# B step of a two-layer-type kernel: where the V-tail matmuls stand, which engine makes Pm, and what the last steps issue

## The chip, the cores and the metric

The kernel runs on one core of a Trainium2 chip. A core has TensorE (PE; its weight loads, PEld, are listed apart since they overlap the matmuls), VectorE (DVE), ScalarE (ACT), GpSimd (POOL) and SyncE (SP), which here only issues DMAs. The metric is device time in microseconds (us) for one execution of the whole program. Engines run their own instruction streams in order and meet through semaphores.

## The reference

The program applies four layers to x of 2048 tokens by 640: A, B, A, B, each as x + layer(layernorm(x)). Layer A is a linear-memory attention in 4 segments of 512 tokens and 32 heads of 20. Layer B, which the change touches, is a transformer with a recurrent memory: 64 segments of 32 tokens, and 8 memory rows that go from segment to segment.

```python
for s in range(n_seg):                       # 64
    xs = x[:, s * 32:(s + 1) * 32, :]
    h = jnp.concatenate([mem, xs], axis=1)   # 8 + 32 rows
    q, k, v = h @ Wq, h @ Wk, h @ Wv         # 32 heads of 128
    scores = where(mask, q @ k.T * scale, -1e9)
    o = (softmax(scores) @ v) @ Wo
    mem = o[:, :8, :]
    outs.append(o[:, 8:, :])
```

So a segment's rows can be projected ahead of time, but its 8 memory rows are known only when the segment before is through all of attention and the output projection. That recurrence sets the order of everything in B.

## The kernel before, in words

Layer B is one Python loop over 64 steps (`for s in range(nsteps)` in `layer_B`), unrolled. In every B layer the order of TensorE, ScalarE, VectorE and GpSimd is the order in which the code issues the instructions: a wrapper (`_OrdNC`) chains each engine's instructions, which is also why all of them carry line 105 in the profile. The DMA issues on SP are placed by the framework's scheduler. An engine may run ahead of the others into a later step as far as its inputs are there.

The columns of step s. A "thin" operand of 32 columns holds the 8 memory rows that enter segment s and the first 24 tokens of segment s + 1. Its projections Ka, Qa, Kb, Qb and Va, Vb (`thin_mm`: 20 matmuls each, four side by side in column groups of 32, five chunks of 128 of the 640 inputs) give the memory rows' K, Q, V for this step and the 24 tokens' K, Q, V for the next.

The tails. The last 8 tokens of each segment are projected apart, for 8 segments (one group T) at a time, as 64 columns. Eight units per group, one per step, make Q and K for 8 heads each (`tail_unit`: 40 matmuls; `tail_evac` stores to DRAM as QKd), and eight V-tail units make V (`vtail_unit`: five chunks of 4 matmuls of 256 columns, side by side; `vtail_evac` stores to VTd). A step reads back its own part: `tails_load` brings Q and K of the tails into the tile tl (one buffer), GpSimd copies them to QZ and KT (`tails_copy`), and `vtails_in` loads V. In a step s the unit is that of group (s + 1) // 8 + 1; from step 55 on there is no further group, so steps 55 to 63 of each B layer have no unit.

One step, in order of issue on TensorE: Ka, Qa, Kb, Qb; transposes TPak, TPaq, TPbk, TPbq of their copies; the scores (tiles SP, in two groups a and b, preceded by a matmul that adds the mask); Va, Vb; the first 6 of the 8 tail heads; the transposes of the probabilities (PTP, by matmul with an identity, from two tiles: Px for the 32 token columns, Pm for the 8 memory columns); the last 2 tail heads; P times V (OTP); half a chunk of the deferred output projection (OPSd); the output projection OPS (64 matmuls); the other half of OPSd; and the turn.

The softmax runs beside Va, Vb and the tails: VectorE takes the maxima and subtracts them, ScalarE makes the exponentials E, VectorE sums them, takes the reciprocals rs and multiplies: first Pm (12 groups of 8), then Px (groups 0 to 7, then 8 to 11). PTPa needs groups 0 to 7, PTPb groups 0 to 3 and 8 to 11. ScalarE copies PTPa to PTa, VectorE PTPb to PTb.

The turn puts the new memory rows into the next thin operand: ScalarE copies OPS to msb in three parts, TensorE sums and transposes each by tiny matmuls (MT), VectorE copies each MT into the first 8 columns of HX, and the next Ka can begin with chunk 0 as soon as the first copy is there. Between the three MT groups the code issues the five chunks of the V-tail unit as 2, 1 and 2 (`vtail_some`).

PSUM: five buffers (`b_ps`) go round for all tiles named here except TPbq and the tail unit (which share one), OPS and OPSd.

GpSimd has little in a step: the copies QZ (two) and KT of `tails_copy`, the copy OTdef of the attention output for the deferred projection, and now and then a tiny power for the layer norm.

Of the kernel before, what the change touches and what calls it, by code (L numbers as in the profile page):

```python
# [29 lines left out]
NCH = 5  # L30
# [512 lines left out]
def layer_B(nc, tc, C, W, x_src, xb_src, x_dst, mem0, B_Wv, B_Wo, nsteps=64, out_bf16=False, tag=""):  # L543
    SCB = 1.0 / math.sqrt(128.0)
    nc_raw = nc
    nc = _OrdNC(tc, nc_raw, engines=ORDER_ENGINES)
    NG = nsteps // 4
    NT = nsteps // 8
    QKd = tc.dram_tile([nsteps, 128, 512], BF16, name=f"b_QKd{tag}")
    VTd = tc.dram_tile([nsteps, 8, 4096], BF16, name=f"b_VTd{tag}")  # L550
    with ExitStack() as ctx:
# [21 lines left out]
        def ps_tile(shape, dtype, name):  # L573
            return pp.tile(shape, dtype, name=name, tag="ps")


        Px = st.tile([128, 12, 32], BF16, name="b_Px")
        Pm = st.tile([128, 12, 32], BF16, name="b_Pm")
# [39 lines left out]
        def evac(eng, dst, src, scale=None):  # L618
            if eng == "act":
                if scale is None:  # L620
                    nc.scalar.copy(dst, src)
                else:
                    nc.scalar.activation(out=dst, in_=src, func=ACT.Copy, scale=scale)
            else:
                if scale is None:
                    nc.vector.tensor_copy(dst, src)
                else:
                    nc.vector.tensor_scalar(out=dst, in0=src, scalar1=scale, scalar2=None, op0=ALU.mult)
# [12 lines left out]
        def ln_spread(g):  # L641
            xt = ln_xt.pop(g)
            tps = ps_tile([128, NCH, 4, 32], BF16, "b_lntps")
            for c in range(NCH):
                nc.tensor.transpose(tps[:, c, :, :].rearrange("p i t -> p (i t)"), xt[:, 128 * c:128 * c + 128], C.identb[:])
            HX[g] = hp.tile([128, NCH, 4, 32], BF16, name="b_HX", tag="HX")
            T, half = divmod(g, 2)
            if half == 0:
                TX[T] = tx.tile([128, NCH, 8, 8], BF16, name="b_TX", tag="TX")
            nc.scalar.copy(HX[g][:, :, :, 8:32], tps[:, :, :, 0:24])  # L650
            nc.scalar.copy(TX[T][:, :, 4 * half:4 * half + 4, :], tps[:, :, :, 24:32])
# [27 lines left out]
        def alloc_seg(s):  # L679
            QT[s] = w2.tile([128, 32, 32], BF16, name="b_QT", tag="QT")  # L680
            KT[s] = w2.tile([128, 32, 40], BF16, name="b_KT", tag="KT")

        def tails_load(s):
            tl = bx.tile([128, 2, 32, 8], BF16, name="b_tl", tag="tl")
            nc.sync.dma_start(tl[:].rearrange("p a h t -> p (a h t)"), QKd[s])
            return tl
# [14 lines left out]
        def tail_unit(T, k, i0, i1, shared=False):  # L701
            proj, hg = divmod(k, 4)
            Wt = W.wk if proj else W.wq
            if i0 == 0:
                if shared:
                    tail_ps[0] = ps_tile([128, 8, 64], F32, "b_tail")
                else:
                    tail_ps[0] = po.tile([128, 8, 64], F32, name="b_tail", tag="tail")
            ps = tail_ps[0]
            for i in range(i0, i1):  # L710
                h = 8 * hg + i
                for c in range(NCH):
                    nc.tensor.matmul(ps[:, i, :], lhsT=Wt[:, c, 128 * h:128 * h + 128], rhs=TX[T][:, c, :, :].rearrange("p s t -> p (s t)"),
                                     start=(c == 0), stop=(c == NCH - 1))

        def tail_evac(T, k, eng, home=None):
            proj, hg = divmod(k, 4)
            pool_, tg = home or (wk, "tu")
            tu = pool_.tile([128, 8, 8, 8], BF16, name="b_tu", tag=tg)
            evac(eng, tu[:].rearrange("p s h t -> p h s t"), tail_ps[0][:].rearrange("p h (s t) -> p h s t", t=8),  # L720
                 None if proj else SCB)
            o = 256 * proj + 64 * hg
            nc.sync.dma_start(QKd[8 * T:8 * T + 8, :, o:o + 64].rearrange("s p f -> p s f"), tu[:].rearrange("p s h t -> p s (h t)"))

        def vtail_unit(T, k, c0=0, c1=NCH, ps=None):
            b4, ch = divmod(k, 2)
            if ps is None:
                ps = ps_tile([128, 256], F32, "b_vtail")
            for c in range(c0, c1):
                for q in range(4):  # L730
                    n = 2 * b4 + q // 2
                    nc.tensor.matmul(ps[32 * q:32 * q + 32, :], lhsT=TX[T][:, c, 4 * (q % 2):4 * (q % 2) + 4, :].rearrange("p s t -> p (s t)"),
                                     rhs=W.wv[:, c, 512 * n + 256 * ch:512 * n + 256 * ch + 256],
                                     start=(c == 0), stop=(c == NCH - 1), tile_position=(0, 32 * q), skip_group_check=True)
            return ps
# [122 lines left out]
        for s in range(nsteps):  # L858
            last = (s == nsteps - 1)
            u = s + 1  # L860
            cols = cols_of(u)
            unit = None
            if (s + 1) // 8 + 1 < NT:
                unit = ((s + 1) // 8 + 1, (s + 1) % 8)
            if not last:
                alloc_seg(s + 1)
                tl = tails_load(s + 1)
# [41 lines left out]
            E_ = wk.tile([128, 12, 40], BF16, name="b_E", tag="E0")  # L909
# [11 lines left out]
            def soft_sum(a):  # L921
                nc.vector.tensor_reduce(out=ssum[:, slice(*GR[a])], in_=E_[:, slice(*GR[a]), :], axis=AX.X, op=ALU.add)

            def soft_p(P_, k0, k1, g0, g1):
                nc.vector.tensor_tensor(out=P_[:, g0:g1, 0:k1 - k0], in0=E_[:, g0:g1, k0:k1],
                                        in1=rs[:, g0:g1].unsqueeze(2).to_broadcast([128, g1 - g0, k1 - k0]), op=ALU.mult)

            def p_transp(b):
                ptp = ps_tile([128, 2, 4, 40], F32, "b_PTP")
                sel = C.identb[:, 64 * b:64 * b + 64].rearrange("p (i c) -> p i c", c=32)[:, :, 0:16]  # L930
                for part, P_ in ((1, Pm), (0, Px)):
                    nc.tensor.matmul(ptp[:, part, :, 8:40], lhsT=P_[:, 4 + 4 * b:8 + 4 * b, :].rearrange("p g k -> p (g k)"), rhs=C.identb[:],
                                     start=True, stop=True, skip_group_check=True)
                    nc.tensor.matmul(ptp[:, part, :, 0:8], lhsT=P_[:, 0:4, :].rearrange("p g k -> p (g k)"), rhs=sel,
                                     start=True, stop=True, skip_group_check=True)
                return ptp
# [41 lines left out]
            soft_sum(0)  # L978
            soft_sum(1)
            nc.vector.reciprocal(out=rs[:], in_=ssum[:])  # L980
            soft_p(Pm, 32, 40, 0, 12)
            soft_p(Px, 0, 32, 0, 8)
            soft_p(Px, 0, 32, 8, 12)
            if not last:
                tails_copy(s + 1, tl)
            VH[s] = w2.tile([128, 2, 512], BF16, name="b_Vth", tag="Vth")
# [4 lines left out]

            if ln_ready:
                ln_spread(ln_ready.pop(0))
            if unit:
                tail_unit(unit[0], unit[1], 0, 6)
            ptpa = p_transp(0)
            PTa = wk.tile([128, 2, 4, 40], BF16, name="b_PTa", tag="PTa")
            ptpb = p_transp(1)
# [1 line left out]
            for hf in range(2):  # L1000
                for pt, ptp, eng in ((PTa, ptpa, "act"), (PTb, ptpb, "dve")):
                    evac(eng, pt[:, :, 2 * hf:2 * hf + 2, :], ptp[:, :, 2 * hf:2 * hf + 2, :])
            if unit:
                tail_unit(unit[0], unit[1], 6, 8)
                tail_evac(unit[0], unit[1], "act")
            otf = [ps_tile([128, 2, 4, 40] if j else [128, 4, 40], F32, "b_OTP") for j in range(4)]
            ots = {j: (otf[j][:, 0, :, :], otf[j][:, 1, :, :]) for j in (1, 2, 3)}
# [23 lines left out]
            vps, vc = None, 0  # L1031

            def vtail_some(n_):
                nonlocal vps, vc
                if unit and vc < NCH:
                    vps = vtail_unit(unit[0], unit[1], vc, min(NCH, vc + n_), vps)
                    vc = min(NCH, vc + n_)

            if not last:
                dst = cols_of(u + 1)  # L1040
                msb = wk.tile([128, 320], BF16, name="b_msb", tag="msb")
                parts = ((0, 1), (1, 3), (3, NCH))
                for ca, cb in parts:
                    nc.scalar.copy(msb[:, 64 * ca:64 * cb], ops[:, 64 * ca:64 * cb])
                for pi, (ca, cb) in enumerate(parts):
                    mt = ps_tile([128, cb - ca, 8], F32, f"b_MT{pi}")
                    for c in range(ca, cb):
                        for q in range(4):
                            o = 64 * c + 32 * (q % 2)
                            nc.tensor.matmul(mt[32 * q:32 * q + 32, c - ca, :], lhsT=msb[:, o:o + 32], rhs=selm[:, q // 2, :],  # L1050
                                             start=True, stop=True, tile_position=(0, 32 * q), skip_group_check=True)
                    nc.vector.tensor_copy(dst[:, ca:cb, 0:8], mt[:])
                    vtail_some((2, 1, NCH)[pi])
            vtail_some(NCH)
            if unit:
                vtail_evac(unit[0], unit[1], vps, "act")
# [107 lines left out]
```

## Time and profile before

| | us |
|---|---|
| time before, median of 3 runs | 2844.14 (2843.91 to 2844.21) |
| profiled execution, its own time | 2838.53 |
| its span, first to last instruction | 2836.8 |
| first B layer, first Ka to step 63 | 461.2 to 1411.3 |
| second B layer, first Ka to step 63 | 1861.3 to 2811.7 |
| PE busy | 2647.7 (93%) |
| PEld busy | 1679.9 (59%) |
| DVE busy | 1676.7 (59%) |
| ACT busy | 1566.2 (55%) |
| POOL busy | 633.4 (22%) |
| TensorE clock granted, mean | 0.974 |

The profile is of one execution. Starts and durations are in us from the first instruction; an instruction's row names its output and inputs by the program's tiles (`b_` for layer B, `a_` for layer A). In the chain of waits each piece is the work that the end of the run waited for, followed back from the last instruction. In the timeline, the bracket at the end of a row is the engine's idle time ahead of it and who ended that. The granted clock is the share of its full speed that TensorE was allowed. Matmuls are pipelined: a matmul's row covers its passage through the array, and the next can start before it ends, so starts, not ends, give the pace.

### The profile page before, as it was taken

To read this page: it belongs to the slowest core of one execution; us is meant where nothing else is said; L and a number is where in the kernel's file an instruction comes from. 1 tells how busy PE (TensorE), PEld (TensorE's weight loads), DVE (VectorE), ACT (ScalarE), POOL (GpSimd) and SP (SyncE) were. 2 spreads that over 40 slices of the span, in tenths; PEclk is the share of its full clock that TensorE was granted. 3 is DMA by queue.
4 is the path that set the end of the run, shared out by engine and by line. 5 is a ranking of instruction groups with operands and counts; after the bars stand their busy time and mean duration, and the time that the engine had idled before them with its cause. 6 is when DMAs were issued, how large, how long until landed. Compare 5 with 4: busy or idle time off the path is not lost.

```text
span 2836.8 us, 145610 instructions
## 1 busy us (share of the span) xinstructions
PE 2647.7 (93%) x64776; PEld 1679.9 (59%) x64776; DVE 1676.7 (59%) x4682; ACT 1566.2 (55%) x3516; POOL 633.4 (22%) x1506
## 2 busy tenths in 40 slices
PE   5899998999999999999979999889999999999998
PEld 2455555666666666665535555556666666666654
DVE  5778864555555555555468878545555555555554
ACT  3777773555555455544438778545555555555543
POOL 3456651000000000000025665410001000000000
PEclk8999999999999999999979999899999999999999
DMA  5110135122211222111130111531111112111110
GB/s 208 60 44 23 36 127 138 42 44 45 45 42 43 44 45 43 43 39 31 24 121 20 57 44 38 181 88 42 41 41 40 41 42 43 42 39 38 38 26 17
DMA packets 322950, 156.42 MB, mean 55 GB/s; under 512 B 245776, under 2 KB 311056, under 8 KB 319248
## 3 DMA queue, kind: packets, MB, share of 16 engines
q1 hardware_dynamic: 320880, 136.63, 18.9%
q8 instruction: 506, 8.29, 1.3%
q10 hardware_dynamic: 1440, 10.49, 1.0%
q14 instruction: 124, 1.02, 0.1%
HBM read 95.65 MB, written 51.38 MB: 52 GB/s over the span
## 4 chain that ended last, share of the span: by engine, by line
PE 61%; DVE 13%; ACT 5%; issue 3%; DMA 2%; POOL 1%; SPq 0%; ACTq 0%; DVEq 0%; POOLq 0%
PE b_OPS L105 11%; PE b_Ka L105 5%; PE b_Kb L105 5%; PE b_Qb L105 5%; PE b_Qa L105 5%; PE b_SP L105 4%; PE b_OTP L105 4%; DVE b_ssum L105 3%; PE b_vtail L105 2%; PE b_tail L105 2%; DVE b_negmax L105 2%; PE b_PTP L105 2%; PE b_OPSd L105 2%; DVE b_SP L105 2%; ACT b_E L105 2%
## 5 line engine op out<-in xcount | busy, mean ns | idle before, releaser
L105 PEld LDWEIGHTS <-b_HX 128*32 128x32 bf16 x15360 | 441.2, 97 | 339.3 <-issue 17.9
L375 DVE TENSOR_REDUCE a_nm<-a_S 128x2 f32<-128x1024 f32 (+3 forms) x512 | 404.1, 812 | 91.8 <-PE a_T L407 69.7
L410 ACT ACTIVATE a_PT<-a_T 128x1024 bf16<-128x1024 f32 (+1 forms) x384 | 340.9, 891 | 51.0 <-PE a_T L407 45.1
L105 POOL COPY b_OTdef<-b_OTsb 128x256 bf16<-128x256 bf16 x128 | 51.2, 400 | 1330.9 <-ACT b_OTsb L105 1315.0
L105 PE MATMUL b_OPS<-b_wo,b_OTsb 128*32 128x320 bf16 x8192 | 318.4, 307 | 8.3 <-issue 5.8
L105 PEld LDWEIGHTS <-b_OTsb 128*32 128x32 bf16 x8192 | 205.7, 98 | 99.2 <-DVE b_OTsb L105 24.4
L412 POOL TENSOR_SCALAR_AFFINE_SELECT a_PT<-a_PT 128x256 bf16<-128x256 bf16 (+1 forms) x384 | 197.6, 517 | 236.6 <-ACT a_PT L410 235.5
L105 DVE CAST b_HX<-b_MT 128x8 bf16<-128x8 f32 x372 | 62.5, 172 | 279.8 <-PE b_MT L105 264.6
L105 ACT CAST b_msb<-b_OPS 128x64 bf16<-128x64 f32 x378 | 69.3, 256 | 245.8 <-PE b_OPS L105 245.8
L105 ACT CAST b_kq<-b_Kb 128x512 bf16<-128x512 f32 x128 | 74.9, 585 | 202.5 <-PE b_Kb L105 202.5
L105 DVE TENSOR_SCALAR b_kq<-b_Qa 128x512 bf16<-128x512 f32 x128 | 88.6, 692 | 126.0 <-PE b_Qa L105 125.5
L105 DVE COPY b_KT<-b_TPak 128x128 bf16<-128x128 bf16 x128 | 28.8, 225 | 225.6 <-PE b_TPak L105 225.6
L105 PE MATMUL b_Va<-b_wv,b_HX 128*32 128x512 bf16 x2520 | 160.7, 380 | 0.0
L105 PE MATMUL b_Vb<-b_wv,b_HX 128*32 128x512 bf16 x2520 | 160.0, 379 | 0.0
L105 PE MATMUL b_Qb<-b_wq,b_HX 128*32 128x512 bf16 x2520 | 159.0, 379 | 0.0
L105 PE MATMUL b_Kb<-b_wk,b_HX 128*32 128x512 bf16 x2520 | 159.0, 379 | 0.0
L105 PE MATMUL b_Ka<-b_wk,b_HX 128*32 128x512 bf16 x2520 | 159.0, 379 | 0.0
L105 PE MATMUL b_Qa<-b_wq,b_HX 128*32 128x512 bf16 x2520 | 159.0, 379 | 0.0
L407 PE MATMUL a_T<-a_q,a_kT 32*128 32x512 bf16 (+3 forms) x1024 | 139.4, 306 | 20.4 <-DVE a_nm L375 14.7
L105 PEld LDWEIGHTS <-b_kq 128*128 128x128 bf16 x2080 | 116.8, 98 | 69.7 <-ACT b_kq L105 55.2
L366 PE MATMUL a_S<-c_negu,c_identb 128*128 128x128 bf16 (+1 forms) x768 | 124.4, 241 | 25.9 <-DVE a_nm L375 15.4
L105 DVE CAST b_OTsb<-b_OTP 128x160 bf16<-128x160 f32 (+1 forms) x384 | 122.4, 374 | 43.0 <-PE b_OTP L105 42.9
(196 smaller groups left out, 5614.8 us busy)
## 6 DMA issues: line engine op xcount, KB each, us to landing
b_QKd<-b_tu SPq DMA_DIRECT2D x128, 128.0 KB
b_tl<-b_QKd SPq DMA_DIRECT2D x128, 128.0 KB
b_wv<-in_B_Wv_dram SPq DMA_DIRECT2D x10, 1024.0 KB
b_wo<-in_B_Wo_dram SPq DMA_DIRECT2D x16, 640.0 KB
b_VTd<-b_vt SPq DMA_DIRECT2D x256, 32.0 KB
b_Vth<-b_VTd SPq DMA_DIRECT2D x512, 16.0 KB
b_XO<-xres SPq DMA_DIRECT2D x256, 30.0 KB
b_wk<-in_B_Wk_dram ACTq DMA_DIRECT2D x5, 1024.0 KB
```

The lines of the kernel that those rows point to most:

```text
L105: r = f(*a, **k)
L366: nc.tensor.matmul(X[:, e, m0:m1], lhsT=C.identb[:], rhs=C.negu[:, 0:(m1 - m0) // 128, :].rearrange("p a k -> p (a k)"), start=True, stop= ...
L375: nc.vector.tensor_reduce(out=nm[:, qc, 2 * pr:2 * pr + 2], in_=X[:, :, o:o + w_], axis=AX.X, op=ALU.max, negate=True)
L407: nc.tensor.matmul(Y[:, e, o:o + w_], lhsT=kT[rows, 128 * kc:128 * kc + 128], rhs=q2[rows, 128 * kc:512], start=True, stop=True, tile_posi ...
L410: nc.scalar.activation(out=PT[:, :, b:b + width], in_=Y[:, :, 0:width], func=ACT.Exp, scale=SC)
L412: nc.gpsimd.affine_select(out=dv, in_=dv, pattern=[[0, 2], [0, diag], [1, 128]], compare_op=ALU.is_ge, fill=0.0, base=0, channel_multiplie ...
```

## The change

Three things change in a step. First, the V-tail unit's chunks are issued as 2 ahead of the turn, then 1, 1 and the rest (one) behind the three MT groups, where before they were 2, 1 and 2 behind them. Second, Pm is made by GpSimd instead of VectorE, issued between the two Px instructions of VectorE, and the transposes take Px before Pm. On GpSimd's queue Pm stands ahead of the step's `tails_copy`. Third, steps 55 to 62 of each B layer, which have no unit, issue the matmuls of one all the same (the tail heads and the V-tail chunks of unit 0 of the last group); nothing copies or reads what they write.

```diff
             unit = None
             if (s + 1) // 8 + 1 < NT:
                 unit = ((s + 1) // 8 + 1, (s + 1) % 8)
+            work = unit or (None if last else (NT - 1, 0))
...
-            def soft_p(P_, k0, k1, g0, g1):
-                nc.vector.tensor_tensor(out=P_[:, g0:g1, 0:k1 - k0], in0=E_[:, g0:g1, k0:k1],
+            def soft_p(eng, P_, k0, k1, g0, g1):
+                eng.tensor_tensor(out=P_[:, g0:g1, 0:k1 - k0], in0=E_[:, g0:g1, k0:k1],
                                         in1=rs[:, g0:g1].unsqueeze(2).to_broadcast([128, g1 - g0, k1 - k0]), op=ALU.mult)
...
-                for part, P_ in ((1, Pm), (0, Px)):
+                for part, P_ in ((0, Px), (1, Pm)):
...
             nc.vector.reciprocal(out=rs[:], in_=ssum[:])
-            soft_p(Pm, 32, 40, 0, 12)
-            soft_p(Px, 0, 32, 0, 8)
-            soft_p(Px, 0, 32, 8, 12)
+            soft_p(nc.vector, Px, 0, 32, 0, 8)
+            soft_p(nc.gpsimd, Pm, 32, 40, 0, 12)
+            soft_p(nc.vector, Px, 0, 32, 8, 12)
...
-            if unit:
-                tail_unit(unit[0], unit[1], 0, 6)
+            if work:
+                tail_unit(work[0], work[1], 0, 6)
...
+            if work:
+                tail_unit(work[0], work[1], 6, 8)
             if unit:
-                tail_unit(unit[0], unit[1], 6, 8)
                 tail_evac(unit[0], unit[1], "act")
...
-                if unit and vc < NCH:
-                    vps = vtail_unit(unit[0], unit[1], vc, min(NCH, vc + n_), vps)
+                if work and vc < NCH:
+                    vps = vtail_unit(work[0], work[1], vc, min(NCH, vc + n_), vps)
                     vc = min(NCH, vc + n_)
 
+            vtail_some(2)
             if not last:
                 dst = cols_of(u + 1)
...
                     nc.vector.tensor_copy(dst[:, ca:cb, 0:8], mt[:])
-                    vtail_some((2, 1, NCH)[pi])
+                    vtail_some((1, 1, NCH)[pi])
             vtail_some(NCH)
```

## The prediction

> **What bounds the kernel now.** I read the page's slices first: TensorE is 93% busy, and nearly all of the span is the two B layers, 64 steps each. I then took their lengths from the busy time of each engine in stretches cut at the first Ka matmul of a step: steps 0 to 54 of each B layer (they have a tail unit), then steps 55 to 62 (they have none).
>
> ```profile
> 461.20:1288.10 826.90, 810.86 (x23874) 540.77 (x23870) 449.08 (x1457) 429.60 (x1124) 73.72 (x229) 1.00 0.20 43
> 1288.10:1411.30 123.20, 112.39 (x3000) 67.92 (x2992) 62.74 (x205) 54.10 (x145) 9.78 (x32) 0.96 0.12 28
> 2687.80:2811.70 123.90, 114.01 (x3001) 68.30 (x2994) 62.73 (x205) 54.01 (x145) 9.78 (x32) 0.94 0.10 25
> ```
>
> The columns are stretch, its length, busy time of PE, PEld, DVE, ACT and POOL, granted clock, DMA share and GB/s. A step with a unit takes 826.9/55 = 15.03 us; one without takes 15.4 and 15.5, although it has 60 matmuls fewer. Cut step by step, these alternate:
>
> ```profile
> 1288.10:1302.70 14.60, 13.36 (x382) 8.14 (x374) 7.51 (x25) 7.07 (x19) 2.09 (x7) 1.00 0.15 39
> ...
> 1317.50:1333.60 16.10, 14.95 (x382) 8.89 (x375) 7.58 (x26) 6.70 (x18) 1.22 (x4) 0.89 0.12 32
> 1333.60:1348.20 14.60, 13.35 (x382) 8.12 (x374) 7.61 (x26) 6.70 (x18) 1.22 (x4) 1.00 0.08 16
> ```
>
> The mean clock of 0.89 over 16.1 us is about 3.5 us at half speed, which costs 1.5 us. No step with a unit has it (1.00 over 826.9 us). Third, one step with a unit on the chain of waits; such steps repeat at 14.82 us, and their mean is 0.21 above that from scattered stalls in instruction issue.
>
> ```profile
> 709.13 0.24 DVE b_rs L105
> 709.37 0.02 issue
> 709.40 0.26 DVE b_Pm L105
> 709.66 0.35 DVE b_Px L105
> 710.00 0.05 issue
> 710.05 0.45 PE b_PTP L105 x6
> ...
> 711.97 2.22 PE b_OPS L105 x64
> ...
> 714.26 0.22 ACT b_msb L105
> 714.49 0.04 issue
> 714.53 0.19 PE b_MT L105 x4
> ```
>
> Two places are not TensorE's own work: the softmax end (VectorE makes Pm, then Px; TensorE waits for Px) and the turn (the first b_MT waits for ScalarE's copy b_msb).
>
> **The V-tail matmuls.** Around the turn the timeline of PE is:
>
> ```profile
> 713.99 0.44 PE L105 MATMUL b_OPSd<-b_wo,b_OTdef 128*32 128x320 bf16 x8
> 714.53 0.19 PE L105 MATMUL b_MT<-b_sel,b_msb 128*32 128x8 bf16 x4
> 714.57 0.39 PE L105 MATMUL b_vtail<-b_wv,b_TX 128*32 128x256 bf16 x8
> 714.78 0.20 PE L105 MATMUL b_MT<-b_sel,b_msb 128*32 128x8 bf16 x8
> 715.21 0.39 PE L105 MATMUL b_Ka<-b_wk,b_HX 128*32 128x512 bf16 x4
> ```
>
> 64 OPS matmuls take 2.22 us, four side by side, so 0.14 a round; OPSd's two rounds from 713.99 leave the array free at 714.26, 0.27 before b_MT. Eight b_vtail matmuls take 714.78 - 714.57 = 0.21 and fit into that gap; nothing is pushed back. From b_MT to Ka is 0.68 now and 0.47 without them. What is late next is the new memory column: Ka needs VectorE's copy of the first b_MT. In the steps without units nothing lies between, and Ka starts 0.47 after b_MT (step length 14.60 against 14.82). Both limits agree, so 0.21 is gained, and no more. The ps slot that the unit takes is freed by OTP copies at 712.5 at the latest; ScalarE's copy of b_vtail ends about 0.2 earlier than now, ahead of Qa, which may take that slot. In about 7 of the 110 steps the gap is already eaten by a stall: 103 x 0.215 = **-22.1 us**.
>
> **The unread matmuls.** They add 960 matmuls in 16 steps and no copy, DMA or wait. Tails 0 to 5 run under the softmax, where these steps idle about 1 us (Vb ends near 8.3 us into a step, b_PTP starts at 9.3); tails 6 and 7 run while b_PTa is copied, since b_OTP starts 10.33 into a step with or without them; the V-tail part has just been shown to fit. So they cost nothing beyond the 14.60, and with the PE load of a unit step the half-clock stretches should go. With the usual 0.21 of stalls: 8 x 14.81 = 118.5 against 123.2 and 123.9, together **-10.1 us**. If the clock still fell, this is 0.
>
> **Pm on GpSimd.** Nothing in before runs Pm there, so it is bounded from rows. *Own time:* GpSimd's two-input rows are 0.27 us (a_NM, 16 elements), 0.45 (a_MZ, 128) and 0.73 (a_am, 320); 96 elements give 0.40, against 0.26 on VectorE. *Start:* in the layer norms GpSimd starts 0.08 after VectorE's result; VectorE's own next instruction starts after 0.035. So Px leads by about 0.045. *Contention:* layer A shows a GpSimd instruction beside a VectorE one with two SBUF inputs:
>
> ```profile
> 376.09 0.67 DVE L286 SCALAR_TENSOR_TENSOR a_phiq<-a_EQ,a_rq 128x512 bf16<-128x512 bf16 x1
> ```
> ```profile
> 376.18 1.08 POOL L412 TENSOR_SCALAR_AFFINE_SELECT a_PT<-a_PT 128x512 bf16<-128x512 bf16 x1 [0.60 <-ACT a_PT L410]
> ...
> 381.15 0.64 POOL L412 TENSOR_SCALAR_AFFINE_SELECT a_PT<-a_PT 128x512 bf16<-128x512 bf16 x1 [1.15 <-ACT a_PT L410]
> ```
>
> Alone (381.15) the select takes 0.64. Started 0.09 into a_phiq it takes 1.08 and ends 0.50 after it: all but its first 0.14 us waits until VectorE is through. Px (inputs E and rs, both in SBUF) is of that kind, so Pm does not run beside Px but behind it. [...]
>
> Worked out on the step above (rs ends 709.36): Px for groups 0 to 7 (0.42) now runs 709.40 to 709.82. Pm has waited since 709.44, takes the port at 709.82 and needs 0.40 - 0.15 = 0.25: 710.07. The second Px waits for it and ends 0.15 later, 710.22 (before: 710.19). b_PTP: Px a at 709.87; Pm a at 710.12 and 710.18, done 0.18 later at 710.36 (before, PTPa was done at 710.29: +0.07 for ScalarE's b_PTa); Px b 710.27, at the array 710.27 and 710.34; Pm b 710.37 and 710.43, done 710.61 (before 710.495: +0.12 for VectorE's b_PTb, which b_OTP's second half and then OPS follow). I take +0.12 in each of 128 steps: **+15.4 us**. Best end, no contention: Pm is ready at 709.84, the second Px at 710.02, the transposes end 0.08 sooner: -10. Worst ends: see the rivals. I take the middle since the rows with the same order of starts (VectorE leads, GpSimd waits) show the waiting one served when the instruction ends, though VectorE's next instruction there read PSUM. Two waits are new. TensorE's transposes wait for GpSimd; behind them stand tails 6 and 7 and b_OTP, which is the shift counted here. VectorE's second Px waits for Pm; behind it stand the copies b_PTb, in the same shift.
>
> On GpSimd's queue Pm now stands ahead of the step's QZ and KT copies, so these run near 710 to 711.2 of the step before their scores, no longer 14 us earlier. They are needed 10 us later; the load b_tl they release goes out that much later too, is wanted a step on, and at a tail boundary the longest wait now (4.5 us) ends 4 us into the step, ahead of Pm. SP's queue: same DMAs, no new wait that can hold it for long. Cost nothing; without that slack each late microsecond would hold b_OTdef and the next Pm.
>
> **Sum.** -22.1 - 10.1 + 15.4 = -16.8. The profiled execution took 2838.5 (span 2836.8), 5.6 under the median of the timed runs, 2844.1; I subtract from the median: **2827**.
>
> **Rivals.**
> - *Pm behind both Px.* VectorE starts the second Px 0.085 before the first ends and may keep the port. Then Pm ends 710.27, the transposes are done 0.25 late: 128 x 0.26 = 33 instead of 15: 2845, no change. For it: back-to-back GpSimd memsets at 1836 held a VectorE instruction for 1.58 us instead of 0.45. Against: in layer A the waiting side was served at the first boundary (a_PT 0.50 behind a_phiq, as above).
> - *Slower: the second Px waits for GpSimd's copies.* QZ, QZ, KT (0.24, 0.24, 0.40 apart) follow Pm at once; if GpSimd keeps the port as in those memsets, one copy makes the step 0.35 later (45 us: 2857), all three about 0.95 (2930 or more). Against: where GpSimd's next instruction reads SBUF (a_PT behind a_xnb at 353.37), VectorE got in first. It decides from 0.25 us per step on, where Pm eats up 32 us.
> - *No contention for Px* (rs is a broadcast): -42, 2802. Against it: a_rd, also with a broadcast input, took 0.38 and not 0.15 at 238.16, beside a GpSimd instruction.
> - *The gap gives nothing* (b_MT is held by the V-tail part, or the new column comes late): +22 on the forecast, 2849.
>
> **Numbers.** Forecast 0.50, Pm behind both 0.20, copies first 0.13, no contention 0.09, gap nothing 0.08. The forecast alone would lie in 2815 to 2836 (Pm's cost 0.06 to 0.18 a step). For 8 in 10 I add the Pm-last and no-gap cases and leave out 2802 and 2857 up: 2812 to 2851. A run of this kernel tells about 0.2% (5.7 us) from no change: faster 0.48 + 0.09 + 0.03 = 0.60; same 0.12; slower 0.13 + 0.10 + 0.05 = 0.28.
>
> **What would show it.** Eight b_vtail matmuls inside the 0.27 before b_MT and Ka 0.47 after it; clock 1.00 in steps 55 to 62; Pm on POOL longer than 0.6 us, ending 0.25 after the first Px, the second Px lengthened to about 0.49. If Pm takes 0.40, contention was wrong; if the second Px keeps 0.285 and Pm ends 0.45 after the first, it went last; a second Px above 0.6 means that copies took the port. Wrong altogether if b_tl waits reappear on POOL ahead of Pm, or if unit steps start to show half clock.

## The result and the profile after

The changed kernel takes 2835.74 us (median of 8 runs, 2832.92 to 2840.20) against 2844.18 for the kernel before on the same chip (8 runs, 2841.62 to 2849.10): a ratio of 0.9969, 95% interval 0.9958 to 0.9980, or 8.4 us less. The forecast was 2827, 17 less. The profiled execution took 2836.99 (span 2835.3) against 2838.53 (2836.8) before.

The busy time by stretches, cut as in the prediction (steps 0 to 54 of the first B layer, steps 55 to 62 of it, the same steps 55 to 62 of the second):

```profile
460.10:1286.70 826.60, 814.95 (x23874) 545.85 (x23866) 448.81 (x1402) 429.87 (x1124) 103.71 (x287) 1.00 0.21 43
1286.70:1406.30 119.60, 118.30 (x3488) 77.48 (x3476) 62.66 (x197) 54.13 (x145) 14.06 (x40) 1.00 0.12 29
2688.70:2808.60 119.90, 118.78 (x3486) 77.38 (x3480) 62.89 (x197) 54.03 (x145) 14.22 (x40) 1.00 0.11 26
```

The stretches without units lost 3.6 and 4.0 us. The first line is the surprise: 826.9 us before, 826.6 now. What was to save 0.1 us in each of its 55 steps has saved nothing. Yet the edits themselves did what they say. TensorE's timeline around the turn:

```profile
714.44 0.46 PE L105 MATMUL b_OPSd<-b_wo,b_OTdef 128*32 128x320 bf16 x8
714.71 0.40 PE L105 MATMUL b_vtail<-b_wv,b_TX 128*32 128x256 bf16 x8
714.99 0.19 PE L105 MATMUL b_MT<-b_sel,b_msb 128*32 128x8 bf16 x4
...
715.39 0.28 PE L105 MATMUL b_vtail<-b_wv,b_TX 128*32 128x256 bf16 x4
715.50 1.25 PE L105 MATMUL b_Ka<-b_wk,b_HX 128*32 128x512 bf16 x20
```

Eight b_vtail matmuls lie in the gap ahead of b_MT, which still starts 0.55 after b_OPSd (0.54 before), and Ka follows b_MT by 0.51 instead of 0.68. The softmax end, from the timelines of VectorE and then of GpSimd (the second b_Px is the second of the x2, and ends at 710.14):

```profile
709.09 0.23 DVE L105 RECIPROCAL b_rs<-b_ssum 128x12 f32<-128x12 f32 x1
709.36 0.78 DVE L105 TENSOR_TENSOR b_Px<-b_E,b_rs 128x256 bf16<-128x256 bf16 x2
710.56 0.56 DVE L105 CAST b_PTb<-b_PTP 128x160 bf16<-128x160 f32 x2 [0.42 <-PE b_PTP L105]
```
```profile
709.49 0.49 POOL L105 TENSOR_TENSOR b_Pm<-b_E,b_rs 128x96 bf16<-128x96 bf16 x1 [11.53 <-ACT b_Vth L105]
709.94 0.58 POOL L105 COPY b_QZ<-b_tl 128x128 bf16<-128x128 bf16 x2
710.47 0.40 POOL L105 COPY b_KT<-b_tl 128x256 bf16<-128x256 bf16 x1
```

To separate the length of a step from what disturbs it, I cut the 108 unit steps 1 to 54 of both layers at the starts of Ka, SP, Vb, rs, PTP, OTP, OPS and MT, and took the 15th percentile of each piece; their sum is called the undisturbed step. It fell from 14.81 to 14.67 us. The mean step did not: 15.02 and 15.03. So the disturbance rose from 0.21 to 0.37 us a step, 108 x 0.153 = 16.5 us. It is no engine's wait for another. This is how it looks, one step of the changed kernel on TensorE:

```profile
1075.56 0.45 PE L105 MATMUL b_OPSd<-b_wo,b_OTdef 128*32 128x320 bf16 x8
1075.83 0.39 PE L105 MATMUL b_vtail<-b_wv,b_TX 128*32 128x256 bf16 x6
1076.83 0.29 PE L105 MATMUL b_vtail<-b_wv,b_TX 128*32 128x256 bf16 x2 [0.61 <-issue]
```

Six of eight b_vtail matmuls run, then TensorE stands still "for issue", in the middle of a group whose inputs are all there. These halts come at one place in the instruction stream. Numbered from 0 in the order of issue, TensorE's instructions (a weight load, a matmul and one of its few semaphore instructions count one each) halt at number 193 of every 256, in every profile of this study. The page of the changed kernel says what is being waited for (busy line, then the row of the DMA queue that brings instructions):

```profile
PE 2667.9 (94%) x65736; PEld 1703.8 (60%) x65736; DVE 1676.5 (59%) x4554; ACT 1567.3 (55%) x3516; POOL 702.8 (25%) x1634
...
q8 instruction: 514, 8.42, 1.3%
```

2 x 65736 instructions are 513.6 blocks of 256; the queue brought 514 transfers, 8.42 MB, 16.4 kB each. Before, 2 x 64776 gave 506.1 blocks and 506 transfers. So TensorE's program comes in blocks of 256 instructions while it runs. From the trace's DMA records: a transfer takes about 1.1 us, and where TensorE had to halt, it went on 1.43 us after the transfer landed (median; 1.35 to 1.48 in the 14 profiles). Nearly all halts in the unit steps fall on one place: the block that follows one entered 10 to 11.5 us into a step. There 256 instructions pass in about 3 to 4 us, and the transfer of the next block begins about 1 us after TensorE has entered the block before. A short block alone is not enough: those entered 8 to 9 us into a step pass in 3.2 us and are followed by no halt, since there the next transfer begins, on average, 0.6 us before the entry (the n-th transfer counted to the n-th block). The halts of over 0.25 us at number 193, summed over the 108 unit steps, are 16.6 us before and 31.0 after. They are most of the "scattered stalls in instruction issue" (108 x 0.21 = 22.7 us) that the prediction carried along as a constant.

What makes them longer? One thing in the trace moved that the prediction had called free. SyncE's queue around the same turn, before:

```profile
711.50 0.38 SPq L723 DMA_DIRECT2D b_QKd<-b_tu  x1
711.94 2.86 SPq L696 DMA_DIRECT2D b_Vth<-b_VTd  x4
714.84 0.43 SPq L685 DMA_DIRECT2D b_tl<-b_QKd  x1
```

with GpSimd's copies of tl near the end of the step, behind b_OTdef:

```profile
712.89 0.53 POOL L105 COPY b_QZ<-b_tl 128x128 bf16<-128x128 bf16 x2
713.36 0.40 POOL L105 COPY b_KT<-b_tl 128x256 bf16<-128x256 bf16 x1
```

and SyncE's queue after:

```profile
710.89 0.32 SPq L685 DMA_DIRECT2D b_tl<-b_QKd  x1
711.53 1.01 SPq L723 DMA_DIRECT2D b_QKd<-b_tu  x1
712.59 2.88 SPq L696 DMA_DIRECT2D b_Vth<-b_VTd  x4
```

GpSimd's copies of tl now run behind Pm (KT ends at 710.87 in the rows of GpSimd further up, at 713.76 before), which frees the only tl buffer there, and b_tl's load (128 KB) leaves ahead of the Vth loads instead of behind them, just as TensorE passes into a new block near 10.5 us into a step.

### The profile page after: what moved, and what is told of

It reads as the page before. It is cut to its first block, busy times and chain, and to the rows that moved or that the text cites. A ratio compares the mean times of both kernels' runs of the same rounds, so it can differ in the third digit from the quotient of the medians.

```text
span 2835.3 us, 147285 instructions
## 1 busy us (share of the span) xinstructions
PE 2667.9 (94%) x65736; PEld 1703.8 (60%) x65736; DVE 1676.5 (59%) x4554; ACT 1567.3 (55%) x3516; POOL 702.8 (25%) x1634
## 3 DMA queue, kind: packets, MB, share of 16 engines
q8 instruction: 514, 8.42, 1.3%
## 4 chain that ended last, share of the span: by engine, by line
PE 54%; DVE 4%; ACT 3%; DMA 2%; issue 1%; POOL 1%; SPq 0%; ACTq 0%; DVEq 0%; POOLq 0%
PE b_OPS L105 7%; PE b_tail L105 4%; PE b_Ka L105 4%; PE b_Qa L105 4%; PE b_Kb L105 4%; PE b_Qb L105 4%; PE b_Va L105 3%; PE b_Vb L105 3%; PE b_SP L105 3%; PE b_OTP L105 2%; PE b_PTP L105 2%; PE b_vtail L105 2%; PE b_OPSd L105 2%; DVE a_nm L375 2%; PE a_QP L276 1%
## 5 line engine op out<-in xcount | busy, mean ns | idle before, releaser
L105 PEld LDWEIGHTS <-b_HX 128*32 128x32 bf16 x15360 | 435.9, 97 | 338.7 <-issue 16.5
L105 POOL TENSOR_TENSOR b_Pm<-b_E,b_rs 128x96 bf16<-128x96 bf16 x128 | 63.5, 496 | 1446.1 <-ACT b_Vth L105 1082.8
L105 PE MATMUL b_OPS<-b_wo,b_OTsb 128*32 128x320 bf16 x8192 | 309.9, 301 | 10.3 <-issue 7.3
L105 DVE TENSOR_SCALAR b_kq<-b_Qa 128x512 bf16<-128x512 f32 x128 | 88.5, 692 | 116.7 <-PE b_Qa L105 114.0
L105 PE MATMUL b_vtail<-b_wv,b_TX 128*32 128x256 bf16 x2880 | 138.9, 271 | 8.0 <-issue 4.8
```

Of the source, the lines that this page charges most:

```text
L105: r = f(*a, **k)
```

## Experiments

Two theories for the 16.5 us. **F**: the gap that the V-tail part filled had been covering late code, so any kernel with that part pays. **D**: the early b_tl slows the fetch of code in the turn. Every ratio is to runs of the kernel before on the same chip. There are three such groups, in which the kernel before took 2837.6, 2837.5 and 2837.4 us; they are marked 1, 2, 3.

**The three parts alone** (group 1). V-tail part only:

```diff
+            vtail_some(2)
             if not last:
...
-                    vtail_some((2, 1, NCH)[pi])
+                    vtail_some((1, 1, NCH)[pi])
```

> Only the V-tail chunks move (2 ahead of the turn, then 1, 1, 1). Two theories of where the change's gain went. Theory F (late code for TensorE): the time that the turn gives up had been covering late instruction blocks; an undisturbed step gets 0.17 us shorter (14.81 to about 14.64), but the stalls at the turn grow by nearly as much, 0.12 to 0.15 us per step with a unit: total 2 to 6 us below before. Theory D (the load b_tl, which now leaves 4 us earlier beside the other loads, slows things at the turn): here b_tl still leaves where it did, so the stalls stay at 0.21 us per step and the total is 17 to 19 us below before.

Pm on GpSimd only, with the transposes' new order:

```diff
-            soft_p(Pm, 32, 40, 0, 12)
-            soft_p(Px, 0, 32, 0, 8)
-            soft_p(Px, 0, 32, 8, 12)
+            soft_p(nc.vector, Px, 0, 32, 0, 8)
+            soft_p(nc.gpsimd, Pm, 32, 40, 0, 12)
+            soft_p(nc.vector, Px, 0, 32, 8, 12)
```

> Only Pm goes to GpSimd, with the transposes taking Px first. Undisturbed step 0.04 us longer (14.85) by the softmax end. Theory F: the gap at the turn is still there to cover late code, so stalls stay near 0.21 us per step: 4 to 6 us above before. Theory D: b_tl leaves early, the stalls grow by 0.15 us per step as in the changed kernel: about 20 us above before.

The unread matmuls only:

```diff
+            work = unit or (None if last else (NT - 1, 0))
...
-            if unit:
+            if work:
```

> Only steps 55 to 62 change: they issue a unit's matmuls unread. Both theories: the half-clock stretches go, these 16 steps take as long as steps with a unit (15.03 us instead of 15.44), 6 to 7 us below before; steps with a unit are unchanged.

And the changed kernel with the copies of tl issued ahead of Pm, so that b_tl leaves behind the Vth loads again:

```diff
+            if not last:
+                tails_copy(s + 1, tl)
             soft_p(nc.vector, Px, 0, 32, 0, 8)
             soft_p(nc.gpsimd, Pm, 32, 40, 0, 12)
             soft_p(nc.vector, Px, 0, 32, 8, 12)
-            if not last:
-                tails_copy(s + 1, tl)
```

> The changed kernel, but GpSimd's copies QZ, QZ, KT are issued ahead of Pm, so that they run one step earlier, right behind b_OTdef, as in before, and b_tl leaves SP behind the b_Vth loads again. Theory F: the stalls stay at about 0.37 us per step, total within 3 us of the changed kernel (8 to 9 below before). Theory D: the stalls fall back to about 0.21, total about 16 us below the changed kernel, 24 below before.

All runs of the study in one table. "Step" is the undisturbed unit step, "halts" the halts at code blocks in the 108 unit steps of the profiled execution, all in us:

```
kernel            group  median    ratio [95%]                  step    halts  b_tl's load
before                   (see above)                            14.81   16.6   late
changed           first  2835.74   0.9969 [0.9958, 0.9980]      14.67   31.0   early
vtail_only        1      2819.71   0.9938 [0.9926, 0.9950]      14.63   15.9   late
pm_only           1      2847.99   1.0036 [1.0024, 1.0048]      14.84   15.9   early
unread_only       1      2828.20   0.9969 [0.9958, 0.9980]      14.81   10.9   late
copies_first      1      2821.58   0.9944 [0.9932, 0.9956]      14.69   17.6   late
vtail_unread      2      2813.98   0.9914 [0.9895, 0.9933]      14.63   16.7   late
tl_late           2      2822.27   0.9939 [0.9916, 0.9962]      14.67   15.9   late
tl_early          2      2828.64   0.9969 [0.9957, 0.9981]      14.65   20.5   early
after_again       2      2822.94   0.9945 [0.9928, 0.9962]      14.67   21.6   early
after_third       3      2819.82   0.9937 [0.9915, 0.9959]      14.67   22.0   early
tl_late_second    3      2814.92   0.9918 [0.9896, 0.9940]      14.67   14.2   late
tl_x2             3      2833.00   0.9996 [0.9980, 1.0011]      14.67   39.7   early, double
tl_late_x2        3      2807.83   0.9889 [0.9868, 0.9909]      14.67   15.3   late, double
```

The V-tail part alone gives 17.9 us, where F had said 2 to 6 and D 17 to 19, and has no more halts than before: F is refuted as it stood. Pm alone costs 10.4 us, of which 4.4 lie in the unit steps (1622.1 to 1626.5 us over the 108) and 4.7 in steps 55 to 62, where the clock is down for longer (0.93 granted in both stretches against 0.96 and 0.94; 123.2 and 123.9 us became 125.9 and 125.9). Pm alone also moves b_tl early, and here D missed: it had said 0.15 us more of stalls a step and about 20 us above before, and the halts stayed at 15.9 us. From here on D is used in an amended form, fitted to this result: the early load makes the code late, but the gap ahead of b_MT, which this kernel keeps, takes the lateness up. So neither the filled gap nor the early load makes halts by itself; whether both together do is what the later runs ask. copies_first, the changed kernel without the early load, gave 16.0 us and few halts; in direction that is D, but D had said 24, and the changed kernel on other chips came to 15.6 and 17.9 (below). The three parts add up to -17.9 + 10.4 - 9.4 = -16.9.

**Separating the load from the copies** (group 2). copies_first moves two things: the load, and the copies, which run behind b_OTdef again instead of beside VectorE's second Px (the two QZ of the step near 710 took 0.53 us in copies_first and 0.58 in the changed kernel). "The port", in the prediction and in two expectations below, is a name for whatever VectorE and GpSimd might share; no run shows a port, only how long their instructions take beside each other. tl_late leaves the copies behind Pm and only orders the load:

```diff
-            nc.sync.dma_start(tl[:].rearrange("p a h t -> p (a h t)"), QKd[s])
+            d_ = nc.sync.dma_start(tl[:].rearrange("p a h t -> p (a h t)"), QKd[s])
+            if vth_last:
+                tc.add_manual_dep(d_.ins, vth_last[-1].ins.name, mybir.DependencyInfo(mybir.DependencyClass.NoSync, mybir.DependencyReason.SCHED_ONLY), reason="order")
...
-                nc.sync.dma_start(VH[s - 1][32 * j:32 * j + 8, :, :],
+                r_ = nc.sync.dma_start(VH[s - 1][32 * j:32 * j + 8, :, :],
                                   VTd[s].rearrange("t (b n e) -> t n b e", b=2, e=512)[:, j, :, :])
+            vth_last.append(r_)
```

> The changed kernel with one edge: b_tl's load is ordered behind the Vth loads of the same turn. The copies stay where the change put them, right behind Pm. Theory D (the early load slows TensorE's code fetch): the excess of a unit step falls from 0.37 to 0.21 to 0.25 us, some -15 us against the changed kernel, ratio to the kernel before 0.991 to 0.993. Rival P (what costs is the copies QZ, QZ, KT behind Pm on the shared port, not the load): the time stays that of the changed kernel, ratio near 0.997.

tl_early goes the other way, from the V-tail part alone, with Pm left on VectorE:

```diff
             if not last:
+                rj = wk.tile([128, 1], F32, name="b_rj", tag="rj")
+                nc.gpsimd.tensor_copy(rj[:], rs[:, 0:1])
                 tails_copy(s + 1, tl)
```

> Part 1 alone (ratio 0.9938 measured), plus a one-element GpSimd copy of rs ahead of the copies QZ, QZ, KT, so that they run behind the softmax and b_tl's load leaves ahead of the Vth loads as in the changed kernel; Pm stays on VectorE. Theory D: the excess of a unit step rises from 0.20 to about 0.35 us, +14 to +18 us against part 1 alone, ratio 0.998 to 1.000. Rival (the slower code needs Pm on GpSimd, by the later softmax or the port): within 4 us of part 1 alone, ratio 0.993 to 0.995; the GpSimd copies themselves may cost 1 to 4 us by the port in either case.

The third is the V-tail part and the unread matmuls, without Pm's move; the fourth the changed kernel itself.

> Parts 1 and 3 together, Pm left on VectorE and everything in its old order there, so that b_tl's load leaves behind the Vth loads as in the kernel before. If only the early b_tl spoils the change (theory D), nothing interacts here: -17.9 of the V-tail alone and -9.4 of the unread matmuls alone add to -27, ratio 0.990 to 0.991, and the excess of a step over its undisturbed length stays near 0.20 us. If the two parts share a gain or the removed gap costs more once the clock is held (rival), the sum falls short, -20 or less, ratio 0.993 or more.

> The changed kernel unaltered, timed on the same chip as the three others: ratio 0.996 to 0.998 as measured, excess of a unit step near 0.37 us.

In halts D came out right in direction in all of them: 15.9 and 16.7 us with the late load, 21.6 and 20.5 with the early one, Pm on GpSimd or not. In size it did not. The changed kernel, whose first profile had 31.0 us of halts and a disturbance of 0.37 a step, has 21.6 and 0.26 here, with a ratio of 0.9945; tl_late has 0.23 a step, as D said, but is not measurably faster beside it (2822.3 and 2822.9), which by the time alone is what rival P had said. vtail_unread gave 23.5 us of the 27 (its ratio of 0.9914 is just above the 0.990 to 0.991, its disturbance of 0.24 above the 0.20). tl_early stood 0.0031 above the V-tail part alone, 9 us across two groups, where D had said 14 to 18 and its rival at most 4; 6.6 of them are in the unit steps (1601.9 to 1608.5 us). One profile each cannot tell an effect of 5 us from chance: the unit steps of the first layer, which unread_only leaves as they were, took 808.5 us there and 812.0 in the profile before.

**The dose** (group 3). So the suspected cause was doubled, early and late, with both single versions beside it on one chip. The wide load also brings the block of the step before:

```diff
-            tl = bx.tile([128, 2, 32, 8], BF16, name="b_tl", tag="tl")
-            nc.sync.dma_start(tl[:].rearrange("p a h t -> p (a h t)"), QKd[s])
+            tw = bx.tile([128, 2, 512], BF16, name="b_tl", tag="tl")
+            s0 = max(s - 1, 0)
+            nc.sync.dma_start(tw[:, s0 - s + 1:2, :], QKd[s0:s + 1].rearrange("n p f -> p n f"))
+            tl = tw[:, 1, :].rearrange("p (a h t) -> p a h t", a=2, t=8)
```

> The changed kernel once more, beside the next three on one chip. So far the waits over 0.25 us at TensorE's code blocks, summed over the 108 unit steps, came to 31.0 us in the changed kernel's first profile and 21.6 us in its second, on another chip, against 15.9 to 17.6 us where b_tl's load leaves late. Theory D expects 20 to 31 us here, and the undisturbed unit step at 14.67 us.

> The kernel with b_tl's load ordered behind the Vth loads once more. Theory D: 15 to 18 us at the code blocks in the unit steps, 5 to 14 us less than the changed kernel beside it, undisturbed step unchanged at 14.67 us. Rival N (the sums differ from run to run for a reason that has nothing to do with the load): no order between the two, both anywhere from 15 to 31 us.

> The changed kernel with b_tl's load doubled at its early place: it also brings the block of the step before, which nobody reads, 128 x 2 x 512 elements in one transfer. Theory D: the load's share of the waits doubles, 26 to 45 us at the code blocks, 5 to 14 us more than the changed kernel beside it. Rival N: no more than the changed kernel, within 3 us. The time itself is not compared, since the wider buffer moves weight loads between the layers.

> The doubled load in its late place, behind the Vth loads. Theory D (what matters is that the load lies beside the fetch of the block that the turn needs): 15 to 20 us at the code blocks, as with the single late load. Rival M (any more bytes beside the step slow the fetches, wherever they lie): as much above the single late load as the doubled early load is above the changed kernel.

The unit stretches (steps 0 to 54 of each layer), columns as above; first after_third, the single early load:

```profile
472.40:1293.00 820.60, 812.24 (x23874) 539.39 (x23870) 448.92 (x1402) 429.61 (x1124) 103.27 (x287) 1.00 0.20 44
1864.80:2686.10 821.30, 811.68 (x23874) 536.64 (x23866) 448.70 (x1402) 429.65 (x1124) 103.26 (x287) 1.00 0.19 41
```

tl_late_second, the single late load:

```profile
462.60:1281.70 819.10, 812.00 (x23875) 535.21 (x23868) 448.88 (x1402) 429.62 (x1124) 103.27 (x287) 1.00 0.20 44
1852.30:2668.10 815.80, 810.84 (x23874) 534.85 (x23870) 448.81 (x1402) 429.62 (x1124) 103.26 (x287) 1.00 0.19 41
```

tl_x2, the double early load:

```profile
456.90:1284.10 827.20, 813.38 (x23875) 541.35 (x23870) 448.63 (x1402) 429.65 (x1124) 103.13 (x287) 1.00 0.23 52
1850.60:2682.20 831.60, 814.01 (x23874) 538.58 (x23866) 448.63 (x1402) 429.74 (x1124) 103.24 (x287) 1.00 0.22 49
```

tl_late_x2, the double late load:

```profile
455.90:1274.00 818.10, 811.79 (x23874) 539.36 (x23866) 448.68 (x1401) 429.60 (x1124) 103.06 (x287) 1.00 0.23 53
1838.80:2656.90 818.10, 811.92 (x23874) 535.29 (x23866) 448.66 (x1402) 429.61 (x1124) 103.27 (x287) 1.00 0.22 50
```

Both stretches together: 1641.9, 1634.9, 1658.8 and 1636.2 us. Same instructions, same DMA share in the two wide kernels, same undisturbed step of 14.67. Doubled late, the load costs 1.3 us (halts 14.2 to 15.3); moved early, 7.0 (22.0); doubled early, 16.9 more (39.7). Of the halts D had said 5 to 14 us less for the late load (7.8) and 5 to 14 more for the double early one (17.7, so more than double). Rival N (chance) said at most 3 us for the double, rival M (any bytes) as much for the late double as for the early one; both fall. This does not rest on single profiles: the two wide kernels differ in the order of this one load alone, and their timed medians are 2833.0 (12 runs, none under 2830.4) and 2807.8 us (4 runs, none over 2809.8), 25.2 us apart. GpSimd's copies stand behind Pm in both, so rival P does not explain it either. The DMA records say how. For the 60 to 62 blocks whose predecessor TensorE enters 10.5 to 11.5 us into a step, where b_tl's load goes out:

```
                 fetch begins  lands    halts of these blocks
                 (us after the predecessor's entry)
before               0.97       2.19        9.1
changed              1.22       2.43       22.0
after_third          1.17       2.25       15.2
tl_late_second       0.94       2.00        7.4
tl_x2                1.49       2.63       34.5
tl_late_x2           0.96       2.08        8.8
```

The early load makes these fetches begin 0.2 us later, the double one 0.55. All 14 profiles fall in line: they begin 0.93 to 0.99 us after the entry in the eight with a late load, 1.08 or more in the five with a single early one (pm_only among them, at 1.09), and latest in tl_x2. And in the kernels with the V-tail part, the halts of these blocks are 6.7 to 11.2 us in the six with a late load, 13.7 to 22.0 in the four with a single early one. With the gap, TensorE was through with the predecessor after 3.64 us, halts taken off; with the V-tail part in the gap, after 3.52 to 3.54. By the 1.43 us measured between landing and use, a fetch must land at 2.1 us; the late load meets it on average (2.00 and 2.08), the early one misses it, and the miss is near what is lost: 60 x (2.63 - 2.1) = 32 us in tl_x2 (34.5), 60 x (2.43 - 2.1) = 20 in the changed kernel's first profile (22.0), 60 x (2.25 - 2.1) = 9 in after_third (15.2). This estimate goes by means and leaves out the spread, which costs 7 to 9 us even where the mean is in time. All other blocks of a step showed no such difference in the four kernels.

## Why the prediction was right or wrong

The direction and the range held. The first measurement, -8.4 us (interval -11.9 to -5.7), is half the forecast of -16.8; the two later ones (-15.6, from -20.4 to -10.8, and -17.9, from -24.1 to -11.6, by the ratios) contain it. So the sum came out near, but three of its terms were mis-sized and a fourth, put at nothing, was missed. That the later runs lie so near the forecast is luck: a cost of Pm that was too high stood against gains that were too high and stalls that were left out.

- **V-tail part, predicted -0.215 a step, measured -0.174.** The gap took the eight matmuls, as said: b_MT's distance to the start of the last OPS matmul stayed 0.67. But Ka follows b_MT by 0.51, not by the 0.47 of the steps without units. Three chunks remain behind the MT groups. Ka's first weight load still starts 0.05 after the copy of the memory column that it needs, but its first matmul starts 0.10 after that copy instead of 0.05, and 0.10 behind the last b_vtail matmul, as it does in the kernel before. The step that failed is "both limits agree": the 0.47 was read where no V-tail matmul stood between. 108 x 0.174 = -18.8.
- **Pm on GpSimd, predicted +0.12 a step, measured +0.035 (pm_only).** The order was the forecast's middle case: Pm started 0.14 into the first Px (0.045 predicted), took 0.496 (median of 128), ended 0.21 after it (0.25 predicted), and the second Px ended 0.15 behind Pm (0.15 predicted), 0.439 long against 0.285 before. One sign that the prediction named did not come: Pm was to take more than 0.6 us. Most of the difference is its later start. And in the one step where Pm started behind the first Px it took 0.41, so running beside Px added only 0.09, where waiting for Px with all but its first 0.15 would have added about 0.14 (an estimate: 0.425 - 0.14 - 0.15). That the second to start waits until the first is through was carried over from layer A's select (1.08 us beside a_phiq, 0.64 alone); here the second Px did so behind Pm (0.439 for 0.285), and Pm behind the first Px was delayed, but by less. GpSimd's copies did not get in ahead of the second Px, and Pm did not go last, so two rivals are out. Where the 0.12 became 0.04: the handover took 0.04 less than predicted (Pm's 0.21 for 0.25), so b_PTb starts 1.24 after the end of rs in the step shown, against 1.17 before, +0.07; and 0.03 of that is made up inside b_OTP, whose second half took 0.41 instead of 0.44, so that the next b_OPSd comes only 0.04 later (2.19 and 2.15 after the end of rs). The step that failed is "which b_OTP's second half and then OPS follow", one for one.
- **Unread matmuls, predicted -10.1, measured -7.6 in the two stretches** together with what the other parts do there. The clock is 1.00 in both, as said, where it was 0.96 and 0.94, and PE is busy for 118.3 and 118.8 us of them, where it was 112.4 and 114.0. That a busier PE holds the clock was the author's estimate from the unit steps; unread_only (PE busy for 117.6 of 119.7 us, clock 1.00) fits it, and no run shows a cause. Alone this part gave 9.4 us in all. The steps are 14.95 and 14.99 long on average, the shortest 14.68, so they lost 0.3 each where the prediction had 0.21; halts of over 0.25 us at number 193 are 0.19 of it. The first step of the second layer fell from 16.42 to 14.52; no other profile shows 16.42, so I don't count it for the change.
- **Stalls, predicted unchanged, measured +16.5, and +5.2 and +5.8 in the two later profiles.** This is the missed term. Two sentences of the prediction failed together: that 0.21 us of stalls a step could be carried over, though I had not asked what they were, and "SP's queue: same DMAs, no new wait that can hold it for long", with the later copies and load put at "Cost nothing". No wait was new, but the order was: the load overtook the Vth loads. The prediction asked whether b_tl would be late for its own reader. It should have asked whom it meets on the way.

Put together for the first profile: -18.8 + 3.8 - 7.6 - 2.2 + 16.5 = -8.3 in the B layers (-2.2 is the two first steps), against 1900.5 - 1892.3 = 8.2 read from the stretches. What lies outside B scatters: the stretch from step 63 to the second layer's first Ka took 450.0 us in the profile before and 456.2 after, 446 to 456 over all profiles, and the lead-in 456 to 472. Times differ by up to 20 us between runs of one kernel in groups 2 and 3, probably for this reason, which is why the readings here go by the unit steps.

Three things stay open. Why the early load cost 14 us of halts in the first profile and 5 to 6 in the two later ones (the fetches took 1.16 us on average there and 1.09 in after_again, but what made them slower isn't shown). Why a load that has left SyncE earlier holds up the start of a code transfer on another queue, beyond that it does. And whether the 2.4 us by which the stretch between the layers is longer on average in the kernels with unread matmuls (453.6 and 451.2, without the two wide ones) belongs to the change.

The V-tail part with the unread matmuls, Pm left on VectorE, beats both kernels at 2813.98, ratio 0.9914; tl_late_second, with all three parts, came to 0.9918. tl_late_x2 is faster still (0.9889), but that comes mostly from outside the B steps: its wider buffer put the loads of b_wv between the layers in another order, and the lead-in and the stretch between are the shortest of the study (455.9 and 446.4 us).

## What to carry to other kernels

The short "issue" gaps that recurred here at number 193 of every 256 instructions were TensorE waiting for its program; before carrying such gaps over as a constant, look at which transfers will lie beside the code fetch after the change, above all at places like the one found here, where a block passed in 3.5 to 3.6 us, halts taken off, and the fetch of the next began 0.9 to 1.5 us after it had been entered. When an edit moves the last reader of a single buffer, follow the load that refills it and what it newly lies beside: here its own data were in good time (GpSimd waited 7.0 us for b_tl in the whole run, 79.3 before), and with the V-tail part moved the halts were 20.5 to 31.0 us all the same, against 14.2 to 17.6 with the load late. And a gap on the critical engine may be cover for such lateness: filling it (vtail_only) and moving a load into it (pm_only) each left the halts at 15.9 us, against 16.6 before, and together, at up to 31.0, took back up to all that both edits had won in these steps.

## What the runs showed of the hardware

- TensorE's instructions come in transfers of 16.4 kB for 256 instructions (514 transfers for 131,472 instructions), each about 1.1 us long, and used 1.43 us after landing where TensorE halts for it. At the place of the halts, 10.5 to 11.5 us into a step, they began 0.9 to 1.5 us after the block before had been entered. In steps of 15 us with some 870 such instructions the halts came to 10.9 to 39.7 us per 108 steps. The halts follow the blocks entered at that place, where 256 instructions pass in 3.5 to 3.6 us, halts taken off; behind those entered 8 to 9 us into a step, which pass in 3.2 us, there were none of over 0.25 us, and there the next transfer began 0.6 us before the entry.
- One 128 KB load, put at the wrong 4 us of a 15 us step, delayed the start of those transfers by 0.2 us, and doubled by 0.55. Some 4 us later, single or double, it left their start at 0.94 to 0.96 us, and doubling it there cost 1.3 us in 1635, no more than profiles of one kernel differ by.
